# Small 32x32 products moved into the first chunk's chain, and the first stretch of a DeltaNet and feed-forward kernel written out with six joint bursts

## The chip, the cores and the metric

The kernel runs on one core of one Trainium2 chip. The metric is the device time of one execution in microseconds (us), lower is better. Four runs of the kernel before gave a median of 680.97 us, from 678.61 to 684.56.

A core has a matrix engine (PE; its weight loads are listed apart, as PEld), a vector engine (DVE), a scalar engine (ACT), a general engine (POOL) and a sync engine (SP), whose queue here issues nearly all DMAs. Each works through its own queue in order. Engines wait for one another by semaphores. PE writes to PSUM, and DVE or ACT read from there.

## What is computed

A delta-rule attention over 4 batches of 8 heads, 768 positions and 48 dimensions, followed by a feed-forward layer with a PReLU (384 to 2048 to 384) on its 3072 rows:

```
k_n = k / (norm(k) + 1e-06)
for t in range(S):
    y[:, :, t] = einsum('bhd,bhde->bhe', q[:, :, t], state)
    v_old = einsum('bhde,bhd->bhe', state, kt)
    state = state + bt * einsum('bhd,bhe->bhde', kt, vt - v_old)
x = y.transpose(0, 2, 1, 3).reshape(B * S, H * D)
h = x @ w_in
out = (maximum(h, 0) + alpha * minimum(h, 0)) @ w_out
```

## The kernel before

The sequence is cut into 12 chunks of 64 positions. A step n is one chunk for one pair of batches, so there are 24 steps and steps 2c and 2c+1 make up chunk c. Within a chunk the recurrence becomes a triangular system for each head. `grams(n)` (L407) forms the 64x64 matrix of k with k. Its 32x32 diagonal blocks are gathered for four steps at a time and inverted on DVE by an elimination (`eliminate`, L499 and L505, a long row of dependent small operations; it starts with POOL's L489). For the first four steps a shorter way is used: DVE eliminates 16x16 blocks only, and `cross` finishes the 32x32 inverses by products of 32x32 tiles on PE. `cross` is a generator in two halves. The first half runs L576 on PE (four products for each of its blocks) and copies the result from PSUM with ACT (L581). The second runs L586 (two for each block) and L593 (four), and DVE adds the results to `turned` and `inverse` (L600, L602). An argument `aside` is called between lots of products. Every product in float32 shows as two PE instructions in the trace.

From the inverses, `placing` (L631 on ACT or L627 on DVE) builds the tiles `diag` and `inv`. `between_1` (L663, then ACT's copy into `mid`, L669) and `between_2` (L677) join the two halves of each 64x64 inverse. `through_state` (L713, L718), `solve` (L743), `outputs` (L756), `next_state` (L772) and `to_ffn` (L795, three transposes, and ACT's copy into `xt`, L797) carry a step to its end. `flips` transposes k and q (L360) and copies them out with ACT (L381, L383).

The feed-forward layer of a chunk is dense work for PE: `ffn_in` has 48 products of 128x256 (L884), six for each of eight blocks that alternate between two PSUM banks (`ps_ffn`). After a block, ACT (L894) and DVE (L896, twice) read it out. Weights come in through staging space and are converted by ACT (L208, L209) and DVE (L218, L223); each converted piece is two parts of the generators `conv_in` and `conv_out`, and a finished piece frees its staging space for the next DMA (L192).

The order of work is written by hand. `weave` interleaves generators by shares, `part` takes a number of parts of one, and `now` runs what it is given at once. Before the first feed-forward work PE has only the chain of chunk 0. `busy(n)` (L1104) puts products there whose results are not used, 512 columns wide for each whole n; these are the fillers. All other PSUM work takes turns in three buffers of two banks (`ps_big`), so that a request waits for the readers of the buffer's last user.

Around the change: `first_chunk` runs the cross products of steps 0 and 1, then the chain of these steps with fillers in it and conversions (`convert`) beside it. After it, one `weave` runs the first hidden layer (`ffn_in(0)`), the cross products of steps 2 and 3 (with more of `ffn_in(0)` between their lots by `aside`), then `ready(2)` and `pair(2)`, the chain of steps 2 and 3, conversions, and `statics(4, 7)`, which prepares k for steps 4 to 7. A second `weave` then runs `ffn_in(1)` beside conversions, `statics(8, 9)` and the beginning of `eliminate(1)`. The products of the first output layer (L926) follow.

Of the kernel before, what the change touches and what calls it, by code (L numbers as in the profile page):

```python
# [41 lines left out]
def kernel(  # L42
# [83 lines left out]
    def load_q(n):  # L126
        if n < N:
            fetch(q, n, q_pad[n % NQ][:, :, 0:D])
# [6 lines left out]
    def load_late(n):  # L135

        if n < N:
            c, bp = steps[n]
            for t in range(2):
                src = k[2 * bp + t, :, c * C : (c + 1) * C, :]  # L140
                src = src.rearrange("(g a) p d -> a p g d", a=2)
                for a in range(2):
                    dst = k_late[n % NKL].rearrange("p (g a) d -> a p g d", a=2)
                    nc.sync.dma_start(out=dst[a][half(t ^ a), :, 0:D], in_=src[a])
# [246 lines left out]
    def now(pieces):  # L391
        for x in pieces:
            x()
# [310 lines left out]
    def through_state(n, p=None, p_y=None):  # L704
        if n >= N:
            return []
        c, bp = steps[n]
        if c == 0:
            rhs_[n] = by_parity(nv[n])
            return []  # L710
        p = region(p, G * (D + C), g=G)
        for g, a, t in quarters():
            nc.tensor.matmul(  # L713
                p[half(t ^ a), a, g], k_t[n][dims(a), g, half(t)], beside[bp][dims(a), t, g]
            )
        p_y = region(p_y, G * D, g=G)
        for g, a, t in quarters():
            nc.tensor.matmul(  # L718
                p_y[half(t), a, g], q_t[n][dims(a), t, g], state[bp][dims(a), t, g]
            )  # L720

        r = work.tile([128, 2, G, D], FP32, name="r")
        v_in = by_parity(nv[n])
        y = work.tile([128, H, D], FP32, name="y")
        rhs_[n], ys[n] = r, y

        def less(to, own, a):
            nc.vector.tensor_tensor(  # L728
                out=r[to, a], in0=v_in[to, a], in1=p[own, a, :, 0:D], op=ALU.subtract
            )  # L730

        return [
            lambda: less(slice(0, 128), slice(0, 128), 0),
            lambda: less(half(0), half(1), 1),
            lambda: less(half(1), half(0), 1),
            lambda: nc.scalar.copy(by_parity(y), p_y),  # L736
            lambda: masked(n, p[:, :, :, D : D + C]),
        ]

    def solve(n, p=None):  # L740
        p = region(p, G * D, g=G)
        for g, a, t in quarters():
            nc.tensor.matmul(  # L743
                p[half(t ^ a), a, g], inv[n % NE][half(t), a * G + g], rhs_[n][half(t), a, g]
            )
        us[n] = work.tile([128, 2, G, D], FP32, name="u")
        return [lambda: nc.vector.tensor_tensor(  # L747
            out=us[n], in0=p,
            in1=stats[n][1][:, 0:3:2, :, None].to_broadcast([128, 2, G, D]), op=ALU.mult,
        )]  # L750

    def outputs(n, p=None):
        c, bp = steps[n]
        p = region(p, G * D, g=G)
        for g, a, t in quarters():
            nc.tensor.matmul(  # L756
                p[half(t), a, g], a_t[n][half(t ^ a), a * G + g], us[n][half(t ^ a), a, g]
            )
        if c == 0:
            ys[n] = work.tile([128, H, D], FP32, name="y")  # L760
            return [lambda: nc.scalar.copy(by_parity(ys[n]), p)]
        return [lambda: nc.vector.tensor_tensor(
            out=by_parity(ys[n]), in0=by_parity(ys[n]), in1=p, op=ALU.add
        )]
# [329 lines left out]
            x()  # L1094
            yield

    PAIR = 6

    def busy(n, p=None):

        p = ps_one() if p is None else p
        while n > 0:
# [3 lines left out]
                k_t[NJ - 1].rearrange("p g i -> p (g i)")[0:ROWS, 0 : x.shape[-1]],  # L1106
            )
            n -= 1

    def pair(n):  # L1110

        both = (n, n + 1)
        for i in both:
            now(through_state(i))
        yield
        for i in both:
            now(solve(i))
            yield
        for i in both:
            now(outputs(i))  # L1120
            now(next_state(i))
            load_late(i + 2)
            load_v(i + 3)
            yield
        for i in both:
            to_ffn(i)
        yield

    READY = 5

    def ready(n):

        both = (n, n + 1)
        for i in both:
            place(i, (0,))
            flips(N, i)
            load_q(i + 2)
        yield
        for i in both:
            now(between_1(i))  # L1140
        yield
        for x in (1, 2, 3):
            for i in both:
                place(i, (x,))
        yield
        for i in both:
            now(between_2(i))
            scale_v(i)
            yield

    def queries():

# [15 lines left out]

        return mask

    def first_chunk(mask, convert):

        both = (0, 1)
        ahead[0] = n_in

        waits, pause = iter([0.5] * 2), []
        middle = cross(
            0, slice(0, 2 * H), edge, half_way, lambda: pause and busy(next(waits, 0), pause[0])
        )
        next(middle)  # L1180
        pause.append(ps_one())
        busy(1, pause[0])
        begin_in(6)
        for i in both:
            scale_v(i)
            mask(i)
        convert(2)
        next(middle)
        busy(1.25)
        place(0, (0,))  # L1190
        place(1, (0,), True)
        for i in both:
            place(i, (1,), True)
            now(between_1(i))
        busy(0.5, ps_ffn())
        for i in both:
            place(i, (2,))
            now(between_2(i))
        for i in both:
            now(through_state(i))  # L1200
            now(solve(i))
        busy(0.5, ps_ffn())
        now(outputs(0))
        convert(4)
        now(next_state(0))
        now(outputs(1))
        now(next_state(1))
        convert(4)
        busy(0.5, ps_ffn())
        for i in both:  # L1210
            to_ffn(i, ps_ffn())
            load_late(i + 2)
            load_v(i + 3)
        ahead[0] = FT * DM
        convert(2)

# [37 lines left out]
    fetch_out, _, conv_out = weights(pieces, stages, ids, out_done)  # L1254
    PARTS_OUT = 2 * len(pieces)

    def in_turn(*gens):
        for _ in range(CROSS):
            for g in gens:
                next(g)  # L1260
                yield

    def chain(*gens):
        for g in gens:
            yield from g
# [35 lines left out]
    def convert(n):  # L1301
        for _ in part(conv_in, n):
            pass

    first_chunk(mask, convert)
    fetch_out(SPACES)
    n = PARTS_IN - n + 10

    first_in = ffn_in(0)
    later = [  # L1310
        cross(0, slice(x * H, x * H + H), edge, half_way, lambda: next(first_in, None))
        for x in (2, 3)
    ]
    weave(
        (first_in, IN_PARTS - 10), (chain(in_turn(*later), ready(2), pair(2)), 2 * CROSS + READY + PAIR),
        (chain(conv_in, part(conv_out, 10)), n), (statics(NJ, 2 * NJ - 1), 2 * NJ + 1),
    )
    fetch_out(len(stages))
    blocks, SOON, LAST = eliminate(1), 12, 6
    weave(  # L1320
# [133 lines left out]
```

## Time and profile before

| | us |
|---|---|
| median of four runs | 680.97 |
| the four runs | 684.56, 678.61, 682.93, 679.00 |
| the profiled execution, its own time | 684.56 |
| its span, first to last instruction | 682.8 |
| mean granted PE clock | 0.984 |
| chain of chunk 0: the first L576 to the first L884 | 28.33 to 55.04 |
| first hidden layer, with steps 2 and 3: to the end of the last of its L884 | about 101.05 |
| second hidden layer: to the first L926 | 128.55 |

The costliest groups of instructions (busy us, mean ns of one; then idle time just before them and what ended most of it):

```profile
L884 PE MATMUL p_ffn<-xt,w_in 128*128 128x256 f32 x1152 | 265.2, 383 | 5.2 <-DVE act L896 2.3
L896 DVE SCALAR_TENSOR_TENSOR act<-act,al_t,p_ffn 128x256 f32<-128x256 f32 x176 | 76.5, 476 | 81.9 <-ACT act L894 81.9
L894 ACT ACTIVATE act<-p_ffn 128x512 f32<-128x512 f32 x88 | 52.4, 596 | 146.3 <-PE p_ffn L884 146.0
L505 DVE TENSOR_TENSOR block<-block,prod 128x30 f32<-128x30 f32 (+9 forms) x150 | 49.9, 333 | 5.1
```

A line names the line of the kernel, the engine, the operation, the tiles written and read, and how many. In lines in order of time (the timeline) the first two numbers are the start and the time from the first start to the last end, in us from the span's start; a bracket at the end gives the idle time before it and what ended that. PE's matrix products are pipelined, so their durations overlap; the distance from one start to the next tells their cost.

### The profile page before, as it was taken

To read this page: it belongs to the slowest core of one execution; us is meant where nothing else is said; L and a number is where in the kernel's file an instruction comes from. 1 tells how busy PE (TensorE), PEld (TensorE's weight loads), DVE (VectorE), ACT (ScalarE), POOL (GpSimd) and SP (SyncE) were. 2 spreads that over 40 slices of the span, in tenths; PEclk is the share of its full clock that TensorE was granted. 3 is DMA by queue.
4 is the path that set the end of the run, shared out by engine and by line. 5 is a ranking of instruction groups with operands and counts; after the bars stand their busy time and mean duration, and the time that the engine had idled before them with its cause. 6 is when DMAs were issued, how large, how long until landed. Compare 5 with 4: busy or idle time off the path is not lost.

```text
span 682.8 us, 21573 instructions
## 1 busy us (share of the span) xinstructions
PE 661.3 (97%) x9359; PEld 575.2 (84%) x9359; DVE 453.3 (66%) x1125; ACT 263.3 (39%) x624; POOL 35.6 (5%) x105
## 2 busy tenths in 40 slices
PE   6999998998999999999999999999999999999997
PEld 4587877766677998998998998998988989989997
DVE  4926688887989869757959757859656345354261
ACT  4815756415455334334334333332243134021110
POOL 6000111101000100001000000000000000000000
PEclk9859999999999999999999999999999999999999
DMA  8816864301342032022021111112111120100000
GB/s 128 238 47 177 202 157 116 90 24 25 66 89 38 13 72 48 11 62 48 15 49 36 23 40 36 26 36 37 25 43 31 30 42 2 29 9 2 23 1 25
DMA packets 110959, 37.69 MB, mean 55 GB/s; under 512 B 104160, under 2 KB 107248, under 8 KB 110864
## 3 DMA queue, kind: packets, MB, share of 16 engines
q1 hardware_dynamic: 109088, 35.81, 24.3%
q8 instruction: 74, 1.21, 0.7%
q10 hardware_dynamic: 1776, 0.49, 0.4%
q14 instruction: 21, 0.17, 0.1%
HBM read 31.56 MB, written 4.72 MB: 53 GB/s over the span
## 4 chain that ended last, share of the span: by engine, by line
PE 80%; DVE 13%; ACT 3%; DMA 1%; issue 1%; ACTq 0%; POOL 0%; SPq 0%; DVEq 0%
PE p_ffn L884 33%; PE p_ffn L948 27%; PE p_big L360 2%; PE p_big L663 2%; PE p_big L713 2%; PE p_big L743 2%; PE p_big L756 2%; DVE prod L499 2%; DVE block L505 2%; PE p_big L407 2%; PE p_big L677 2%; DMA ke<-in_k_dram 1%; DVE block L472 1%; PE p_big L718 1%; PE p_big L772 1%
## 5 line engine op out<-in xcount | busy, mean ns | idle before, releaser
L884 PE MATMUL p_ffn<-xt,w_in 128*128 128x256 f32 x1152 | 265.2, 383 | 5.2 <-DVE act L896 2.3
L884 PEld LDWEIGHTS p_ffn<-xt,w_in 128*128 128x128 f32 x1152 | 213.3, 190 | 35.2 <-ACT sums L894 2.2
L896 DVE SCALAR_TENSOR_TENSOR act<-act,al_t,p_ffn 128x256 f32<-128x256 f32 x176 | 76.5, 476 | 81.9 <-ACT act L894 81.9
L894 ACT ACTIVATE act<-p_ffn 128x512 f32<-128x512 f32 x88 | 52.4, 596 | 146.3 <-PE p_ffn L884 146.0
L948 PE MATMUL p_ffn<-w_out,act 128*128 128x192 f32 x480 | 82.5, 328 | 0.1
L948 PEld LDWEIGHTS p_ffn<-w_out,act 128*128 128x128 f32 x480 | 77.6, 190 | 1.1 <-issue 0.5
L505 DVE TENSOR_TENSOR block<-block,prod 128x30 f32<-128x30 f32 (+9 forms) x150 | 49.9, 333 | 5.1
L499 DVE TENSOR_TENSOR prod<-block 128x30 f32<-128x30 f32 (+9 forms) x150 | 48.9, 326 | 3.3 <-POOL block L489 1.6
L968 DVE TENSOR_TENSOR o_sb<-u,p_ffn 128x192 f32<-128x192 f32 x40 | 13.4, 353 | 52.2 <-PE p_ffn L948 41.9
L797 ACT COPY xt<-p_big 128x384 f32<-128x384 f32 x22 | 10.4, 477 | 75.7 <-PE p_big L795 75.7
L736 ACT COPY y<-p_big 128x384 f32<-128x384 f32 x22 | 10.5, 478 | 51.3 <-PE p_big L718 49.8
L948 PE MATMUL p_ffn<-space_out,sums 128*128 128x192 f32 x160 | 29.4, 327 | 0.0
L948 PE MATMUL p_ffn<-more,sums 128*128 128x192 f32 x160 | 29.3, 326 | 0.0
L948 PE MATMUL p_ffn<-w_out,sums 128*128 128x192 f32 x160 | 27.6, 326 | 0.0
L948 PEld LDWEIGHTS p_ffn<-more,sums 128*128 128x128 f32 x160 | 26.6, 190 | 0.0
L948 PEld LDWEIGHTS p_ffn<-space_out,sums 128*128 128x128 f32 x160 | 26.5, 190 | 0.1
L948 PEld LDWEIGHTS p_ffn<-w_out,sums 128*128 128x128 f32 x160 | 26.3, 190 | 0.0
L689 ACT COPY inv<-p_big 32x256 f32<-32x256 f32 x38 | 13.8, 363 | 29.4 <-DVE u L747 29.2
L631 ACT ACTIVATE diag<-inverse,which 64x128 f32<-64x128 f32 (+2 forms) x60 | 24.2, 405 | 2.1 <-DVE inverse L472 1.4
L728 DVE TENSOR_TENSOR r<-v_raw,p_big 64x192 f32<-64x192 f32 (+1 forms) x66 | 23.2, 352 | 1.0
L349 POOL TENSOR_TENSOR beta_t<-beta_t,rec 128x8 f32<-128x8 f32 x24 | 6.6, 275 | 308.7 <-DVE rec L347 288.1
L332 DVE TENSOR_REDUCE norm<-ksq 128x8 f32<-128x384 f32 x24 | 12.9, 546 | 13.8 <-ACT ksq L330 13.8
(156 smaller groups left out, 966.3 us busy)
## 6 DMA issues: line engine op xcount, KB each, us to landing
w_out<-in_moe_w_in_dram SPq DMA_DIRECT2D x12, 512.0 KB, 5.1
qp<-in_q_dram SPq DMA_DIRECT2D x48, 96.0 KB, 3.0
v_raw<-in_v_dram SPq DMA_DIRECT2D x48, 96.0 KB, 3.0
kl<-in_k_dram SPq DMA_DIRECT2D x96, 48.0 KB, 2.7
out_dram<-o_sb SPq DMA_DIRECT2D x92, 48.0 KB, 1.6
space_out<-in_moe_w_out_dram SPq DMA_DIRECT2D x11, 384.0 KB, 3.3
ke<-in_k_dram SPq DMA_DIRECT2D x43, 96.0 KB, 3.3
w_out<-in_moe_w_out_dram SPq DMA_DIRECT2D x5, 384.0 KB, 3.8
```

Source lines behind the costliest of these rows:

```text
L360: nc.tensor.transpose(p[0:ROWS, g * 128 : (g + 1) * 128], src[:, 2 * g : 2 * g + 2].rearrange("p h d -> p (h d)")[:, 0:ROWS], ident,)
L407: nc.tensor.matmul(p[half(t), a, g], k_t[n][dims(a), g, half(t)], k_t[n][dims(a), g, half(t)])
L499: nc.vector.tensor_tensor(out=prod, in0=r[:, 0:j, j : j + 1].to_broadcast([128, j, n]), in1=r[:, j : j + 1, j + 1 : HB].to_broadcast([128, ...
L505: nc.vector.tensor_tensor(out=r[:, 0:j, j + 1 : HB], in0=r[:, 0:j, j + 1 : HB], in1=prod, op=ALU.add)
L631: nc.scalar.mul(out, x, which[rows, i : i + 1])
L663: nc.tensor.matmul(p[half(t ^ a if changes(n) else t), a, g], right[n % EARLY][half(t), a * G + g : a * G + g + 2].rearrange("p b i -> p ( ...
L689: nc.scalar.copy(to[rows], p[rows])
L728: nc.vector.tensor_tensor(out=r[to, a], in0=v_in[to, a], in1=p[own, a, :, 0:D], op=ALU.subtract)
L884: nc.tensor.matmul(p_h[:, i], w_in[:, t, (f + i) * 128 : (f + i + 1) * 128], xt[:, t], start=(t == 0), stop=(t == KT - 1),)
L894: nc.scalar.activation(g, p_h, ACT.Relu, scale=-1.0)
L896: nc.vector.scalar_tensor_tensor(out=g[:, i], in0=g[:, i], scalar=al_t[:, f + i : f + i + 1], in1=p_h[:, i], op0=ALU.mult, op1=ALU.add,)
L948: nc.tensor.matmul(p, x(i), w(i), start=(i == 0), stop=(i == FP - 1))
```

## The change

Three fillers of half a filler product each (256 columns) are taken out of `first_chunk`, and the four halves of the cross products of steps 2 and 3 are put in: the first half of each in the places of two fillers, the second half of step 2's in the place of the third, and the second half of step 3's after `to_ffn`. The `weave` that ran the first hidden layer is replaced by `second_pair`, which writes the order out: six groups of small products, each of which joins what belonged to two steps or to a step and a gram, with 5, 5, 6, 7, 7, 6 and 12 parts of the hidden layer after them. The flips of steps 4 and 5 and of the queries of steps 2 and 3 come before the first part. `through_state`, `solve`, `outputs` and `next_state` of the two steps share PSUM buffers. `pair`, `ready` and `in_turn` are dropped. The number of products, conversions and loads stays as it was, apart from the fillers.

```diff
-    def first_chunk(mask, convert):
+    def first_chunk(mask, convert, halves):
...
             place(i, (1,), True)
             now(between_1(i))
-        busy(0.5, ps_ffn())
+        next(halves[0])
         for i in both:
             place(i, (2,))
             now(between_2(i))
         for i in both:
             now(through_state(i))
             now(solve(i))
-        busy(0.5, ps_ffn())
+        next(halves[1])
         now(outputs(0))
         convert(4)
         now(next_state(0))
         now(outputs(1))
         now(next_state(1))
         convert(4)
-        busy(0.5, ps_ffn())
+        next(halves[0])
         for i in both:
             to_ffn(i, ps_ffn())
             load_late(i + 2)
             load_v(i + 3)
+        next(halves[1])
...
-    first_chunk(mask, convert)
+    first_chunk(mask, convert, [
+        cross(0, slice(x * H, x * H + H), edge, half_way) for x in (2, 3)
+    ])
     fetch_out(SPACES)
...
-    later = [
-        cross(0, slice(x * H, x * H + H), edge, half_way, lambda: next(first_in, None))
-        for x in (2, 3)
-    ]
-    weave(
-        (first_in, IN_PARTS - 10), (chain(in_turn(*later), ready(2), pair(2)), 2 * CROSS + READY + PAIR),
-        (chain(conv_in, part(conv_out, 10)), n), (statics(NJ, 2 * NJ - 1), 2 * NJ + 1),
-    )
+    convert_on = chain(conv_in, part(conv_out, 10))
+
+    def alongside(products, pieces, *gens):
+        weave((part(first_in, products), products), (part(convert_on, pieces), pieces), *gens)
+
+    def second_pair():
+
+        n = 2
+        both, x = (n, n + 1), NJ
+        squares(x)
+        squares(x + 1)
+        for i in range(2):
+            place(n + i, (0,))
+            flips(x + i, n + i)
+            load_early(x + i + NKE)
+            load_q(n + i + 2)
+        now(weigh(x))
+        now(weigh(x + 1))
+        alongside(5, 3)
+        for i in both:
+            now(between_1(i))
+        now(grams(x))
+        squares(x + 2)
+        alongside(5, 3, (chain(*(placing(i, (1, 2, 3)) for i in both)), 6))
+        for i in both:
+            now(between_2(i))
+        now(grams(x + 1))
+        for i in both:
+            scale_v(i)
+        flips(x + 2, N)
+        load_early(x + 2 + NKE)
+        now(weigh(x + 2))
+        alongside(6, 3)
+        y = ps_big()
+        pieces = []
+        for i in range(2):
+            pieces += through_state(n + i, None, y[:, :, i * G * D : (i + 1) * G * D])
+        now(pieces)
+        squares(x + 3)
+        alongside(7, 3)
+        y = ps_big()
+        pieces = []
+        for i in range(2):
+            pieces += solve(n + i, y[:, :, i * G * D : (i + 1) * G * D])
+        now(pieces)
+        now(grams(x + 2))
+        flips(x + 3, N)
+        load_early(x + 3 + NKE)
+        now(weigh(x + 3))
+        alongside(7, 3)
+        pieces = []
+        for i in both:
+            y = ps_big()
+            pieces += outputs(i, y[:, :, 0 : G * D]) + next_state(i, y[:, :, G * D : 2 * G * D])
+        now(pieces)
+        for i in both:
+            load_late(i + 2)
+            load_v(i + 3)
+        alongside(6, 3)
+        for i in both:
+            to_ffn(i)
+        now(grams(x + 3))
+        alongside(IN_PARTS - 36, 4)
+
+    second_pair()
```

## The prediction

> **What bounds the kernel now.** I read the page first: engine totals, then the chain that ended last.
>
> ```profile
> PE 661.3 (97%) x9359; PEld 575.2 (84%) x9359; DVE 453.3 (66%) x1125; ACT 263.3 (39%) x624; POOL 35.6 (5%) x105
> ...
> PE 80%; DVE 13%; ACT 3%; DMA 1%; issue 1%; ACTq 0%; POOL 0%; SPq 0%; DVEq 0%
> ```
>
> PE (the matrix engine) is 97% busy and carries 80% of the chain, so work or waiting taken off PE in the changed stretch should reach the end unless another engine holds it there. Next I read busy times by stage (columns: PE, PEld, DVE, ACT, POOL, granted clock, DMA share, GB/s). The stages are: chain up to the first filler that goes, rest of the chain, first hidden layer, second hidden layer.
>
> ```profile
> 28.33:43.88 15.55, 15.55 (x395) 11.15 (x395) 8.09 (x20) 5.16 (x10) 0.00 (x0) 0.55 0.40 88
> 43.88:55.04 11.16, 10.54 (x269) 9.06 (x269) 5.94 (x13) 3.05 (x8) 0.00 (x0) 0.71 0.16 43
> 55.04:101.05 46.01, 45.14 (x1023) 35.33 (x1023) 31.77 (x80) 29.67 (x67) 6.31 (x16) 1.00 0.75 186
> 101.05:128.55 27.50, 25.03 (x181) 21.05 (x181) 24.27 (x70) 16.08 (x34) 4.24 (x10) 1.00 0.41 104
> ```
>
> ACT has 29.67 and DVE 31.77 of 46 us in the third stage, so neither binds on average; their order may. The clock is low in the first two. One-microsecond slices give 0.94 at 29–30, 0.50 from 30 to 50 and 0.82 at 50–51: half speed from 29.9 to 50.4. Then PE in order of time, the three fillers of the change and the first W_in product:
>
> ```profile
> 43.80 1.22 PE L1104 MATMUL p_ffn<-k_t,ident 112*128 112x256 f32 x2
> 44.95 3.52 PE L677 MATMUL p_big<-diag,mid 64*64 64x32 f32 x62
> ...
> 50.24 0.74 PE L1104 MATMUL p_ffn<-k_t,ident 112*128 112x256 f32 x2
> ...
> 53.06 0.70 PE L1104 MATMUL p_ffn<-k_t,ident 112*128 112x256 f32 x2
> ...
> 55.04 0.70 PE L884 MATMUL p_ffn<-xt,w_in 128*128 128x256 f32 x2 [0.62 <-ACT xt L797]
> ```
>
> And the stretch after it:
>
> ```profile
> 56.04 0.70 PE L884 MATMUL p_ffn<-xt,w_in 128*128 128x256 f32 x2
> 56.67 0.44 PE L576 MATMUL p_big<-turned,sums 32*32 32x16 f32 x32
> 57.04 0.70 PE L884 MATMUL p_ffn<-xt,w_in 128*128 128x256 f32 x2
> ...
> 62.26 0.68 PE L586 MATMUL p_big<-act,inverse 32*32 32x16 f32 x32
> ...
> 78.64 1.12 PE L677 MATMUL p_big<-diag,mid 64*64 64x32 f32 x32 [0.22 <-ACT diag L631]
> ...
> 86.21 1.00 PE L713 MATMUL p_big<-beside,k_t 48*64 48x112 f32 x32 [0.65 <-DVE right L413]
> ...
> 109.54 2.83 PE L884 MATMUL p_ffn<-xt,w_in 128*128 128x256 f32 x12 [1.85 <-ACT sums L894]
> ```
>
> Each lot of 32x32 products sits between W_in products, and PE waits in four places (last bracket). The wait at 109.54 is DVE's: its L896 stands behind L499 of the elimination, which waits for POOL's L489 until 108.19.
>
> **Part 1: fillers out, 32x32 products in.** A W_in product (two PE instructions) costs 0.44 us back to back (24 instructions from 121.96 to 127.24: 5.28). From 56.04 to 57.04 are one product and one lot: the lot costs 1.00-0.44 = 0.56, though its own work is 0.37 (chain row); the switch between shapes is some 0.17. An L586 lot costs 62.87-60.34-4x0.44 = 0.77. Eight lots at 0.56 and two at 0.77: **6.0 us leave the stretch.** The fillers' chain rows, 1.15, 0.67 and 0.63, free 2.45.
>
> What comes in: 64 instructions of L576 at half clock, by 1.83 for 128 of L593 there (0.92; if they ran like L586 there, 0.97 for 32, it were 1.9): I take 0.95, since L576 uses four quadrants as L593 does. The second 64 at full clock, 2x0.37 and a switch: 0.85. Twice 32 of L586 and 64 of L593, 0.61+2x0.37: 2.7, with a switch 2.8. **Sum 4.6.**
>
> New wait: the third set needs a PSUM buffer that L780 on DVE reads. L780 stands behind two conversions and ended at 53.5 and 54.0; PE would be there at 53.1. I take 0.4 (bounds 0 and 0.9). PE queues the transposes of y behind it. In return the xt copies on ACT (54.13 to 55.0) lie under the fourth set and 16 transposes (L360), which move ahead of the first W_in product; PE's 0.74 us gap there goes. First W_in product: 53.1+0.4+1.4+0.7+1.4+1.75 = **58.75**, with all 32x32 products and both steps' flips done.
>
> **Part 2: six joint bursts.** L663, L677, L407, L713/718, L743 and L756/772 formed eleven bursts among W_in products; now six. Five switches at 0.17: **0.85 saved**. The W_in count (48) and conversions (22 halves) are the same. The waits at 78.64 (0.38 with its pipeline end) and 86.21 (0.65) go. L887–L897's work is unchanged. On SP the loads of q move from 71.9 to about 60, ahead of ke loads that land well before use; loads of kl move behind w_out pieces and are needed a chunk later: nothing. POOL keeps its order: nothing.
>
> But ACT's queue changes. Between the xt copies (end about 56.3) and the copy into diag that step 3's L677 needs stand 8 conversion halves at 0.70 (start to start 54.87 to 55.59), 3 squares at 0.43, 4 flip copies at 0.47, 5 placements at 0.42, 4 norms at 0.23, two mid copies at 0.35, one L894 at 0.5, two L652 at 0.2: 13.4 us, so **69.7**. The copy for step 2 is done 2.65 earlier, at 67.05. PE has from 58.75: five products 2.2, L663 and L407 2.55, five products 2.2, two switches: ready at 66.0. It waits 1.05, runs L677 for 1.1, and waits 1.55 until 69.7: **2.6 us of new wait** where before it was 0.38. Bounds: 0, if ACT keeps ahead, and 4, if it also waits for DVE's norms. From 70.65 follow 38 products (16.8), L407 three times (1.9), L713/718 (2.7), L743 (1.25), eight L360 (0.95), L756/772 (2.15), L795 (0.65), five switches (0.85): the first hidden layer ends at 97.9, not 101.05.
>
> **Given back or kept later.** The last gram now has twelve products behind it before the second hidden layer, not four, so the elimination's start on DVE and POOL moves by more than PE: the same rows one after another put L499 at 104.15, not 108.19 (-4.0). PE loses 0.55 and 1.3 waiting for L896 around it, against 0.62 and 2.0 now. The third block of the layer starts at 105.45, not 109.54; past it the order is the same.
>
> **Sum.** Off: 2.45+6.0+0.85, gaps 0.74+0.38+0.65, and 0.8 around the elimination: 11.9. On: 4.6+0.4+2.6 = 7.6. Net **-4.2**, and -4.1 by the walk; I take -4.1. The profiled execution took 684.56 (span 682.8, 1.8 around it), so 680.5 there. It is the slowest of four; their median is 680.97. On that scale: **676.9**.
>
> **The clock, against the change.** Between 53.5 and 58.75 PE would run only 32x32 products and transposes. The row: the clock fell at 29.9, after a stretch (26.5 to 29.9) of 0.64 us of filler, 1.22 idle and 1.5 of L576. Yet it stayed up in 84.5 to 87.9, with some 0.3 of dense work and 1.9 of 48x64 products. So a fall near 57 is possible, not certain.
> The Trainium skill, "TensorE: Matmul & The Clock Gate", section "What's actually happening", has the clock judged in windows of about 3.4 us, half after an idle one; the 20.5 us of half clock here are six such. By it a single fall would cost 1.7 us as an estimate.
> The same page, section "Part 4: PE-mode transpose", says that transposes do not count as PE work in the same way, which speaks against this change; no run here shows it.
>
> **Rivals.** (a) *The clock falls near 57.* L360 took 1.03 for four at half clock against 0.44, a 128x256 product 1.15 against 0.63. Flips and the first five products then add 3.8, or 6 if L663 is slow too; 2.6 of it lies under ACT's wait, so the cost is 1.3 to 3.3. With 2: 678.9.
> (b) *Slower: the clock does not rise at 50.4*, because the filler at 43.9 no longer helps. L756/772 then cost 3.7 instead of 2.15 (L407's 1.13 against 0.62), the two last sets 4.0 instead of 2.8, L795 1.5, flips 4.1: with five slow products some 8.4, less 2.6 under ACT's wait: +5.9, so +1.8 net: 682.8. It decides once PE comes to the second L677 after 73.7. For it: fillers are what filled the chain. Against: in the 3.4 us before the rise PE ran L677 and L743 alone.
> (c) *The gain is swallowed at the elimination*: L499 stays near 107–108 because DVE (24.27 of 27.5 us busy) gets no earlier: 0 to -1.5, 680.2. Against: DVE idled 14 of 46 us in the stretch before.
> (d) *ACT does not bind*: another -2.6, 674.3. For it: before, ACT waited 3.23 us for PE in this stretch. Against: the sum of rows.
> That the change does something else is excluded: the built order has no such fillers and six bursts.
>
> **How the numbers follow.** Forecast 0.45, (d) 0.15, (a) 0.20, (c) 0.10, (b) 0.10. The four runs before spread by 6 us, so a median of few moves by 2 either way. Range 672.5 (d, less 2) to 683 (b). One per cent, about what a measurement can tell from no change, is 6.8 us: faster than 674.2 needs (d) or a lucky forecast, 0.20; slower than 687.8 needs more than (b), 0.06; within, 0.74.
>
> **What would show it.** Right: first L884 at 58 to 59.5 with clock 1.0; PE waits of 1 to 1.6 us before each L677, released by ACT's L631; L499 about 4 us earlier. Wrong: half clock past 51 (b) or after 57 (a); no wait at L677 (d); L499 within 1 us of 108 (c).

## The result and the profile after

The changed kernel took 682.63 us (median of 43 runs, 679.86 to 687.29); the kernel before, on the same chips, 679.47 us (64 runs, 677.00 to 685.83). The ratio is 1.0037, 95% interval 1.0025 to 1.0049: a loss of some 2.5 us, small but clear of the noise, where 4.1 us of gain was forecast. Three runs of the experiments below, each over 1.5% slower than the fastest of its kernel, are left out of the ratios and mean clocks. The profiled execution took 680.9 us, with a span of 679.2.

The page of the changed kernel first: the engines' totals, PE's instruction queue (packets, MB, share), and the chain that ended last.

```profile
PE 655.7 (97%) x9353; PEld 576.4 (85%) x9353; DVE 454.4 (67%) x1125; ACT 264.2 (39%) x624; POOL 35.0 (5%) x105
...
q8 instruction: 74, 1.21, 0.7%
...
PE 80%; DVE 11%; ACT 3%; SPq 2%; issue 2%; DMA 1%; POOL 0%; POOLq 0%
```

PE's share of the chain is what it was. "issue" has gone from 1% to 2%: that is time in which an engine waited for nothing that the profile shows, and stops of PE are among it. The queue line will explain them: 74 packets of 16 KB each, 1.21 MB in all, bring PE's instructions. The trace has 2 x 9353 products and weight loads of PE and 209 other instructions of its queue, nearly all on semaphores: 18915 in all, so a packet is a block of some 256.

Busy times by stage (the same columns as before the change). The kernel before in two profiles, that of the prediction and a second one taken later, whose clock was full all through; then the changed kernel. In each the first row runs from the first L663 to the first L884 (the rest of the first chunk's chain), the second to the first L926. (In the second profile of before the first row begins 0.22 us ahead of its first L663, at 37.25, so the chain is 12.24 us there.)

```profile
40.25:55.04 14.79, 14.17 (x334) 12.63 (x333) 5.94 (x13) 3.42 (x9) 0.00 (x0) 0.66 0.12 34
55.04:128.55 73.51, 70.17 (x1202) 56.38 (x1203) 56.05 (x149) 45.75 (x101) 10.54 (x26) 1.00 0.62 155
```

```profile
37.03:49.49 12.46, 10.31 (x333) 8.83 (x332) 7.13 (x17) 3.58 (x10) 0.00 (x0) 1.00 0.31 101
49.49:122.97 73.48, 70.34 (x1203) 56.55 (x1203) 55.80 (x148) 45.95 (x101) 10.48 (x26) 1.00 0.61 150
```

```profile
36.49:59.99 23.50, 19.51 (x662) 18.30 (x663) 11.48 (x27) 7.91 (x18) 0.00 (x0) 0.72 0.46 132
59.99:124.77 64.78, 62.46 (x867) 53.30 (x867) 52.16 (x136) 41.74 (x92) 9.96 (x26) 0.97 0.58 144
```

The stretch gave what was forecast and a little more: 73.5 to 64.8, -8.7 us. The chain took it all back: +8.7 against the first profile of before (14.79), +11.3 against the second (12.24). PE is idle for 4.0 of its 23.50 us, and its clock is 0.72 there. Past the first L926 all three profiles take the same 554.2 to 554.4 us. PE of the changed kernel in order of time, in this chain, shows the idle time (bracket):

```profile
36.49 2.06 PE L663 MATMUL p_big<-diag,right 64*64 64x32 f32 x64 [0.42 <-ACT diag L631]
38.47 0.73 PE L576 MATMUL p_big<-turned,sums 32*32 32x16 f32 x64
39.13 1.06 PE L677 MATMUL p_big<-diag,mid 64*64 64x32 f32 x29
41.73 1.19 PE L677 MATMUL p_big<-diag,mid 64*64 64x32 f32 x33 [1.54 <-issue]
...
45.95 0.72 PE L576 MATMUL p_big<-turned,sums 32*32 32x16 f32 x37 [0.78 <-issue]
...
50.97 0.66 PE L593 MATMUL p_big<-inverse,act 32*32 32x16 f32 x56
53.22 0.24 PE L593 MATMUL p_big<-inverse,act 32*32 32x16 f32 x6 [1.59 <-issue]
53.39 1.40 PE L795 MATMUL p_ffn<-ident,y 128*128 128x128 f32 x6
...
56.54 1.10 PE L360 MATMUL p_big<-ident,ke 128*112 128x128 f32 x4
...
59.99 2.53 PE L884 MATMUL p_ffn<-xt,w_in 128*128 128x256 f32 x10
```

Three times PE stops inside a burst, in the middle of products of one kind that all have their operands: 1.54, 0.78 and 1.59 us, 3.9 in sum. Counted from the start of the program, with PE's matrix products, weight loads and semaphore instructions together, the first instruction after each stop is number 1473, 1729 and 2241. Each leaves 193 when divided by 256 ("193 modulo 256"), so they follow the fifth, sixth and eighth end of a block. In the trace's DMA records the fifth, sixth and eighth packet of PE's instruction queue land at 40.29, 44.47 and 51.97, and PE goes on 1.43, 1.48 and 1.25 us later. What ends each stop is the arrival of its block. One-microsecond slices around the first and the third stop (same columns; the clock is the third number from the end):

```profile
40.00:41.00 1.00, 0.19 (x7) 0.07 (x3) 0.00 (x0) 0.33 (x1) 0.00 (x0) 1.00 0.00 0
41.00:42.00 1.00, 0.28 (x9) 0.28 (x10) 0.00 (x0) 0.00 (x0) 0.00 (x0) 1.00 0.00 0
42.00:43.00 1.00, 1.00 (x50) 1.00 (x49) 0.42 (x1) 0.00 (x0) 0.00 (x0) 1.00 0.00 0
43.00:44.00 1.00, 0.92 (x47) 0.82 (x42) 0.90 (x2) 0.00 (x0) 0.00 (x0) 0.67 0.06 16
...
52.00:53.00 1.00, 0.00 (x0) 0.00 (x0) 0.96 (x3) 0.00 (x0) 0.00 (x0) 1.00 0.00 0
53.00:54.00 1.00, 0.78 (x10) 0.76 (x10) 0.77 (x3) 0.00 (x0) 0.00 (x0) 0.79 0.62 106
```

After each of these two the clock falls: half from 43.3 to 50.2 and again from 53.6 to 60.4. A third fall, 70.7 to 74.1, lies in the stretch, behind a wait of 0.94 us for ACT. Nor is the low clock one execution's chance. The mean clock over the changed kernel's runs is 0.983 and never above 0.990; of 107 runs of the kernel before in the comparisons below 49 were at 0.997 or more, with a mean of 0.995. Half clock goes with time: the runs of before at 0.997 or more have medians of 678.2 to 678.8 us, those below 0.990 some 684 (681.4 in one comparison). By (1 - clock) x 2 x 680 the mean clocks are 23 us of half clock a run against 7, and over the runs of either kernel one us of it goes with 0.2 to 0.3 us of time: 3 to 5 us. Continued to no half clock at all, the straight line through the changed kernel's runs comes to 677.8 us, those through the four sets of runs of before to 678.2 to 678.9. By this estimate the two kernels would take about the same at full clock, and the loss goes with the clock. The profile of before that the prediction was read from (clock 0.984, 684.56 us) was thus of the rarer kind: 20 of the 107 are below 0.990.

### The profile page after: what moved, and what is told of

It is laid out like the page before. It is cut to its first block, busy times and chain, and to the rows that moved or that the text cites. A ratio compares the mean times of both kernels' runs of the same rounds, so it can differ in the third digit from the quotient of the medians.

```text
span 679.2 us, 21569 instructions
## 1 busy us (share of the span) xinstructions
PE 655.7 (97%) x9353; PEld 576.4 (85%) x9353; DVE 454.4 (67%) x1125; ACT 264.2 (39%) x624; POOL 35.0 (5%) x105
## 3 DMA queue, kind: packets, MB, share of 16 engines
q8 instruction: 74, 1.21, 0.7%
## 4 chain that ended last, share of the span: by engine, by line
PE 80%; DVE 11%; ACT 3%; SPq 2%; issue 2%; DMA 1%; POOL 0%; POOLq 0%
PE p_ffn L884 32%; PE p_ffn L948 27%; PE p_big L360 3%; PE p_big L713 2%; PE p_big L756 2%; PE p_big L743 2%; DVE prod L499 2%; PE p_big L663 2%; DVE block L505 2%; PE p_big L1102 2%; PE p_big L677 2%; SPq L120 1%; PE p_big L718 1%; PE p_big L772 1%; PE p_big L407 1%
## 5 line engine op out<-in xcount | busy, mean ns | idle before, releaser
L884 PE MATMUL p_ffn<-xt,w_in 128*128 128x256 f32 x1152 | 261.4, 383 | 3.4 <-DVE act L896 2.5
L884 PEld LDWEIGHTS p_ffn<-xt,w_in 128*128 128x128 f32 x1152 | 216.0, 191 | 33.9 <-ACT act L894 3.1
L499 DVE TENSOR_TENSOR prod<-block 128x30 f32<-128x30 f32 (+9 forms) x150 | 48.9, 326 | 3.3 <-POOL block L489 1.6
L780 DVE TENSOR_TENSOR beside<-beside,p_big 48x384 f32<-48x384 f32 (+1 forms) x36 | 19.8, 550 | 2.9 <-PE p_big L772 2.7
L713 PE MATMUL p_big<-beside,k_t 48*64 48x112 f32 x704 | 21.3, 259 | 0.0
```

The source lines that it names most:

```text
L499: nc.vector.tensor_tensor(out=prod, in0=r[:, 0:j, j : j + 1].to_broadcast([128, j, n]), in1=r[:, j : j + 1, j + 1 : HB].to_broadcast([128, ...
L713: nc.tensor.matmul(p[half(t ^ a), a, g], k_t[n][dims(a), g, half(t)], beside[bp][dims(a), t, g])
L780: nc.vector.tensor_tensor(out=x, in0=x, in1=p[rows], op=ALU.subtract)
L884: nc.tensor.matmul(p_h[:, i], w_in[:, t, (f + i) * 128 : (f + i + 1) * 128], xt[:, t], start=(t == 0), stop=(t == KT - 1),)
```

## The experiments

The theory formed from the traces: PE's instructions arrive in blocks of 256, and where it uses them up faster than they come (128 products with their 128 loads take 1.4 us in L576 and, by 64 in 2.0, some 4 us in L677 at full clock) it stops at the end of a block. The change adds 640 short instructions to the chain, two and a half blocks, and the stops bring the clock down with them. The rivals: the half fillers kept the clock up and are missed; products that use little of the array lower the clock; the joint stretch is itself no gain; the stops belong to some place and not to a count.

**The parts alone.** First the four halves of `cross` in the chain, the three half fillers out, and the order of the stretch as before:

```diff
-        busy(0.5, ps_ffn())
+        next(halves[0])
...
-        (first_in, IN_PARTS - 10), (chain(in_turn(*later), ready(2), pair(2)), ...
+        (first_in, IN_PARTS), (chain(ready(2), pair(2)), READY + PAIR),
```

> The four halves of the 32x32 products in the chain, the old order of the stretch after it. Theory S (PE's instruction supply: blocks of 256 PE instructions, and the chain uses them up faster than they arrive): the loss is here, 1.004 to 1.010 of before, with PE stalls of 0.7 to 1.6 us inside bursts, at every 256th instruction. Rival J (the written-out order with joint bursts costs, by its waits for ACT): part 1 alone is a gain, 0.993 to 0.997.

682.55 us; ratio 1.0051 (1.0025 to 1.0077), mean clock 0.983. This part alone loses as much as the whole change. Its profile has two stops in the chain, in the same bursts as the changed kernel's first and third:

```profile
41.98 2.02 PE L677 MATMUL p_big<-diag,mid 64*64 64x32 f32 x34 [1.05 <-issue]
54.62 0.29 PE L593 MATMUL p_big<-inverse,act 32*32 32x16 f32 x6 [2.35 <-issue]
```

Then the rest of the change: the chain with its fillers as before, the lots of steps 2 and 3 among ten W_in products, the six joint bursts.

```diff
-        next(halves[0])
+        busy(0.5, ps_ffn())
...
-        alongside(IN_PARTS - 36, 4)
+        alongside(IN_PARTS - 46, 1)
...
+    weave((chain(*(part(g, 1) for g in later), ...), 4), (part(convert_on, 3), 3))
     second_pair()
```

> Fillers and the chain as before, the 32x32 products of steps 2 and 3 with ten hidden-layer products between their lots, then the written-out order with six joint bursts. Theory S: the order itself is worth its fewer switches and gaps less ACT's wait, 0.997 to 1.001, no stall inside a burst of the chain. Rival J: 1.003 or more, with waits of 1 us or more before each L677.

684.39 us; 1.0035 (0.9998 to 1.0071), clock 0.990: inconclusive. It shows no gain by itself, though its two runs with a clock of 1.0 took 676.45 and 677.56 us, against the 678.6 of before at 0.997 or more. In its profile two stops (0.46 and 0.53 us) now fall into the lots of steps 2 and 3, which stand closer together than in the kernel before.

**Are the fillers missed?** The three half fillers out of the kernel before, and nothing in their place:

```diff
-        busy(0.5, ps_ffn())
```

> Before without its three half fillers in the chain, nothing in their place. Rival K (the fillers hold the clock up, and their loss is what costs): 1.003 or more, and half clock for longer than before. Theory S: their own 1.6 to 2.4 us are saved in part, since PE then waits for ACT and DVE there, 0.997 to 1.000.

680.14 us; 0.9987 (0.9959 to 1.0016), clock 0.993 against 0.994 for before. They are not missed. Nor do they help when they are put back, into the changed kernel behind three of the halves:

```diff
         next(halves[0])
+        busy(0.5, ps_ffn())
```

> The changed kernel with the three half fillers kept, each behind the half that took its place. Rival K: the clock stays up and the time falls below the changed kernel's, 0.996 to 1.001 of before. Theory S: the fillers give the instruction supply 0.6 us each, stalls shrink by about as much as the fillers take, 1.002 to 1.006 of before.

683.31 us; 1.0055 (1.0028 to 1.0083), clock 0.986. Stops of 0.38 and 1.85 us remain. By both, the rival of the missing dense work falls.

**The kernel before once more**, for a profile at full clock.

> The kernel before, for a second profile: most of its runs show a mean granted clock of 0.995 and more, the first profile 0.984. All theories: L884 of the first hidden layer starts 5 to 8 us earlier than 55.04 if the clock holds, and the first L926 at 122 to 125. Theory S: with the chain at full clock one or two stalls of some 1 us appear at 256-instruction marks even here.

678.95 us. It gave the stages shown above, and stops in its own chain too:

```profile
38.56 1.25 PE L663 MATMUL p_big<-diag,right 64*64 64x32 f32 x34 [0.19 <-issue]
46.75 0.37 PE L756 MATMUL p_big<-u,a_t 64*64 64x48 f32 x9 [1.03 <-issue]
```

Numbers 1217 and 1729: 193 modulo 256 again. The first profile of before has none. At half clock PE eats its instructions more slowly (L677 took 3.52 us there, 2.00 here), so the prediction was read from the one kind of execution that hides this cost.

**The supply by itself.** The first fillers replaced by 256 products of 32x32 by 16 columns, 1024 instructions, whose results are not used:

```diff
-    busy(BUSY)
+    for x in range(64):
+        for i in range(4):
+            nc.tensor.matmul(p[quad(i), x % 32], ident[quad(i), quad(i)], ident[...])
```

> Before with the eight wide fillers, where PE waits for the elimination anyway, replaced by 256 products of 32x16 (1024 PE instructions, results unused): measures the supply by itself. Theory S: they take 12 to 16 us, with a stop of 1 to 2.5 us at every 256th instruction. Without a limit of supply: 6 us, by 128 in 1.54, and no stops.

699.12 us (one run). PE in order of time:

```profile
25.32 1.90 PE L1298 MATMUL p_big<-ident 32*32 32x16 f32 x128 [3.09 <-issue]
30.42 1.90 PE L1298 MATMUL p_big<-ident 32*32 32x16 f32 x128 [3.20 <-issue]
33.88 1.90 PE L1298 MATMUL p_big<-ident 32*32 32x16 f32 x128 [1.55 <-issue]
37.88 0.30 PE L1298 MATMUL p_big<-ident 32*32 32x16 f32 x7 [2.10 <-issue]
```

Runs of exactly 128 products and 128 loads, 1.90 us of work at half clock (it rose at 66.7 us only), then 1.55 to 3.20 us of nothing: from start to start 3.5 to 5.1 us a block. The DMA records show where the time goes. The fetch of each such block begins 1.1 to 2.8 us after PE has gone into the block before, takes 1.0 to 1.3 us, and PE goes on 1.3 to 1.5 us after the landing. This is the price of a block that nothing hides.

**Many short or few long, in the fillers' places.** Unused products in place of the three half fillers, the real ones left in the stretch: first 112 of 32x32 by 16 columns (448 instructions), then, in place of these, 11 of 32x32 by 512 columns (44; the second diff is against the first). The sets behind the transposes of y, which the expectations name, were not built.

```diff
-        busy(0.5, ps_ffn())
+        tiny(32)
```

> Before with its three half fillers replaced by as many 32x16 products as the changed kernel has there, results unused (32, 32, 48 products, and 48 behind the transposes of y), and the real ones left in the stretch. Theory S: stalls of 1 us and more appear in the chain and the mean clock falls to 0.980 to 0.987 as in the changed kernel; 1.006 to 1.012. Rival K (only missing dense work lowers the clock): as the kernel without fillers, clock 0.993, 1.002 to 1.005 for the added work.

```diff
-                nc.tensor.matmul(p[quad(i), b], edge[quad(i), 2 * H + b], turned[0][...])
+            nc.tensor.matmul(p[x], ident[x, x], src[x])
```

> The same places filled with 32x32 products of 512 columns (3, 3, 5, and 5 behind the transposes; 32 PE instructions in all instead of 640), as long as the small ones within some tenths of a us and with as little of the array in use. Theory S: no added stall, clock 0.992 or more, 1.000 to 1.004. Rival A (it is the little of the array in use that lowers the clock, not the number of instructions): clock 0.980 to 0.987, 1.004 to 1.009.

The short ones: 692.46 us, 1.0163 (1.0137 to 1.0190), more than expected, clock 0.984. The long ones: 681.64 us, 1.0033 (1.0011 to 1.0056), clock 0.994 as before. The chain of the first has a stop of 1.31 us in L756 and one among the added products, shown here; the chain of the second has only the one in the second row:

```profile
55.92 0.30 PE L1115 MATMUL p_ffn<-turned,sums 32*32 32x16 f32 x6 [3.51 <-issue]
```

```profile
45.53 0.49 PE L756 MATMUL p_big<-u,a_t 64*64 64x48 f32 x17 [0.30 <-issue]
```

Both use tiles of 32x32. The long ones take more time than the fillers (4.0 us against 2.1), which is about their ratio, and leave the clock alone. So small tiles by themselves do not lower it; with many short instructions, and their stops, it is lower.

**Count or place?** 64 unused products early, to move every later instruction along the count:

```diff
-    busy(BUSY)
+    tiny(64)
+    busy(BUSY - 0.5)
```

> The changed kernel with 64 unused 32x16 products (128 instructions, counting weight loads and multiplications) ahead of the fillers that lie behind the queries' products, and half a filler less there, so that every later instruction is counted 128 higher. Theory (PE's instructions come in blocks of 256, and it stops where a block ends): the stops move 128 instructions up the program, to the counts 1473, 1729, 1985 and 2241 again, which now lie in the first L576 burst or the end of L663, in L743, in L756/L772 and in the L586/L593 set after it; no stop stays at the 30th L677, the 28th L576 or the 57th L593. Their sum stays between 2 and 4.5 us, and the time with them: ratio to the kernel before 1.002 to 1.007, mean clock of the runs below 0.989. Rival (the stops belong to these bursts: a PSUM bank, an operand, a wait that the profile does not show): they stay at the 30th L677, the 28th L576 and the 113th instruction of L593, whatever the count.

> The kernel before without the three half fillers, with the same 64 unused products ahead of the first fillers and half a filler less there. Theory: the block ends move from L663, L743 and the second L756 (0.28, 0.26 and 1.11 us of stops without the shift) to the first half of L663 or L677 and to the first L756, and the fifth one out of the chain into W_in products; four block ends in the chain instead of five. Stops of 0 to 1.2 us instead of 1.65; first W_in product within 0.5 us of where it would be without them; ratio 0.995 to 1.000. Rival (stops belong to places): 1.65 us of stops at the same lines and ratio 0.9987 as without the shift.

A product is two multiplications and two loads, so 64 were 256 instructions, not 128: a whole block, and the ends of blocks fell on the same places as without them. The added products also write over a part of the first chunk's products of queries and keys before these are masked, so that both kernels compute something else there, with the same work in the same order. The times: 685.71 us, 1.0100 (1.0065 to 1.0136), and 682.81 us, 1.0069 (1.0039 to 1.0099). Of the three old places of the changed kernel only the third stopped again (number 2497, 1.25 us). What is new is a stop in the added products themselves, behind those of the queries (the kernel without fillers):

```profile
26.15 0.30 PE L1156 MATMUL p_ffn<-ident 32*32 32x16 f32 x7 [4.33 <-issue]
```

3.63 us in the other, both at number 705. Count or place was left open. Half as many in the middle of the first fillers, in their buffer, settled it:

```diff
+    p = ps_one()
+    busy(BUSY / 2, p)
+    tiny(32, p)
+    busy(BUSY / 2 - 0.5, p)
```

> The changed kernel with 32 unused 32x16 products in the middle of the first fillers and half a filler less there. A 32x16 product is two multiplications and two weight loads, so these are 128 instructions, half a block of 256 (the 64 of the shifted kernels were 256, a whole block, so there the block ends fell on the same places as without them). Theory (PE stops where a block of 256 instructions ends): the stops are again at counts of 193 modulo 256 and so at new places: the end of the L663/L576 set, L743, L756/L772, L586/L593 near their start and the second L593 set; none at the 30th L677, the 28th L576 or the 113th instruction of the L593 set. Ratio to the kernel before 1.001 to 1.007, mean clock below 0.990. Rival (the stops belong to the places): one at each of the three old places, at counts of 65 modulo 256.

685.45 us; 1.0077 (1.0050 to 1.0104), clock 0.982. PE in the chain:

```profile
37.26 0.53 PE L593 MATMUL p_big<-inverse,act 32*32 32x16 f32 x30 [1.54 <-issue]
...
44.69 3.52 PE L677 MATMUL p_big<-diag,mid 64*64 64x32 f32 x62
...
49.97 1.05 PE L576 MATMUL p_big<-turned,sums 32*32 32x16 f32 x64
...
58.45 0.82 PE L593 MATMUL p_big<-inverse,act 32*32 32x16 f32 x44 [1.06 <-issue]
```

L677 and L576 run through, the third old place too, and the stops are at numbers 1217 and 2497, both 193 modulo 256, in other bursts: the first in the products of steps 0 and 1, the second in the last set of L593. All 36 stops inside a burst that the profile puts down to "issue", from 20 to 85 us in all the profiles of this study, are at 193 modulo 256. The stops go by the count, and each ends 1.2 to 1.6 us after the packet of the same number has landed. Not every end of a block stops, and the expectation named some bursts that ran through. In all 17 traces, at over 1200 ends of blocks, PE never goes into a block sooner than 1.2 us after its packet has landed; where the packet came early enough, PE runs through.

> The kernel before without the three half fillers, with the same 32 unused products in the middle of the first fillers. Theory: stops only at counts of 193 modulo 256; the ends of blocks move to L586 or its filler, L593, the first part of L677 and the first L756/L772, and one leaves the chain. Stops of 0 to 1.2 us in sum against 1.65 without the shift; ratio 0.995 to 1.000, clock 0.993 or more. Rival (places): stops in L663, L743 and the second L756 as without the shift, ratio 0.9987.

The same in the kernel without fillers: 682.45 us, 1.0029 (1.0006 to 1.0052), clock 0.989. One stop of 1.54 us at number 1217 instead of 1.65 us in three. The expected gain did not come: the one stop lies earlier (35.2 to 36.8), and the clock is half from 36.4 to 50.1, nearly to the end of the chain.

**Half the dose.** Only the first two sets (L576) in the chain; L586 and L593 among six W_in products behind it:

```diff
-        next(halves[0])
-        next(halves[1])
...
+    aside[0] = lambda: next(first_in, None)
+    weave((chain(*(part(g, 1) for g in halves)), 2), (part(convert_on, 2), 2))
     second_pair()
```

> The changed kernel with only the first two sets (the L576 products, 256 instructions) in the chain; the L586 and L593 sets stand among six W_in products behind it, ahead of the joint bursts. Theory (each block of 256 instructions added to the chain costs a stop of 1 to 2 us and, through the clock, as much again): between the kernel before and the changed one, ratio 0.999 to 1.003, mean clock 0.985 to 0.992, stops of 1 to 2.5 us in the chain. Rival (the stretch of 32x32 products and transposes without dense work between 50 and 60 us is what lowers the clock, and the first two sets cost nothing): half clock no later than 51 us, mean clock of the runs 0.993 or more and the ratio at most 0.998, as the prediction's gain in the stretch then shows.

681.17 us; 1.0028 (1.0006 to 1.0049), clock 0.988, stops of 0.48, 1.05 and 0.39 us: between the two kernels, as the theory had it, though the interval holds the changed kernel's 1.0037 too.

**The joint stretch with neither the halves nor the fillers in the chain** (the second kernel above, less its three half fillers):

```diff
-        busy(0.5, ps_ffn())
```

> The part of the change that needs no products in the chain: the three half fillers out, the chain otherwise as before; then the 32x32 products of steps 2 and 3 among ten W_in products, and the six joint bursts. Theory (the chain's added instructions are the loss; leaving out the fillers costs nothing): ratio 0.996 to 1.001, mean clock 0.990 or more; L926 (the elimination's end) by 1 to 2 us earlier than with the fillers in the same program. Rival (the joint stretch itself is no gain: ACT's queue or the clock after it gives back what the shape switches save): 1.002 or more, with the clock's mean at 0.988 as with the fillers.

680.75 us; 1.0008 (0.9977 to 1.0040), clock 0.986. Inconclusive: neither the clock of the theory (0.990) nor the time of the rival (1.002).

**Does a stop by itself lower the clock?** The kernel before, with ACT's first copy into `diag` made five times (same values), so that PE waits before L663 with no instruction added to it:

```diff
+        for _ in range(5):
             place(0, (0,))
```

> The kernel before with ACT's first copy into diag made five times (same values) ahead of L663, so that PE idles there about 1.7 us longer, with no instruction more on PE. Theory 1 (any stop of this length in the chain lowers the clock, as the stops at block ends would): PE's idle time before L663 is 1.5 to 2.2 us; half clock afterwards in most runs, mean clock 0.990 or less, ratio 1.004 to 1.008. Theory 2 (the stop costs itself only, and what lowers the clock is the longer run of short instructions): mean clock 0.993 or more, ratio 1.002 to 1.003. If the clock lies between, both have a part.

683.34 us; 1.0051 (1.0027 to 1.0076), mean clock 0.9905 against 0.9954 for before. None of its 12 runs is above 0.994; 13 of the 25 of before are at 0.997 or more. The wait, and the slices behind it:

```profile
38.59 2.23 PE L663 MATMUL p_big<-diag,right 64*64 64x32 f32 x64 [2.38 <-ACT diag L631]
```

```profile
39.00:40.00 1.00, 1.00 (x42) 1.00 (x40) 0.00 (x0) 0.24 (x1) 0.00 (x0) 1.00 0.07 16
40.00:41.00 1.00, 1.00 (x25) 0.94 (x22) 0.00 (x0) 0.27 (x2) 0.00 (x0) 0.66 0.00 0
41.00:42.00 1.00, 1.00 (x4) 0.35 (x6) 0.00 (x0) 1.00 (x3) 0.00 (x0) 0.50 0.00 0
```

The wait is 2.2 us longer than in before (0.22), and the kernel is 3.7 us slower by the medians. So a stop costs its own length and, through 6.8 us of half clock (40.3 to 47.1), something like half as much again: in the profile the chain behind the wait, from the first L663 to the first L884, took 13.7 us with 0.2 of stops in it, against 12.2 with 1.2 of stops at full clock. The interval of the ratio (1.8 to 5.2 us) doesn't fix this second part; the clocks of the runs do show it.

No kernel here beats the kernel before: the best, 0.9987 without the fillers, has 1 in its interval.

## Why the prediction was wrong

The change went the other way than forecast. That the time still lies in the stated range is luck: the upper end, 683, stood there for rival (b), a clock that does not rise, and not for what happened. Step by step:

- *"Sum 4.6" for the 32x32 products that come in.* **This step failed.** It priced 640 instructions by the time that PE works on them, in part by rows at half clock. With their operands there and PE free, they also need to be fetched, a wait that the sum puts at nothing. From first start to the next burst the four sets took 0.66, 2.03, 2.94 and 1.82 us, 7.5 in sum, 2.4 of it stops; a third stop, of 1.54, fell into L677. In all the profile has 3.9 us of stops in the chain; before at full clock has 1.2. The forecast had the first W_in product at 58.75, 18.5 us after the first L663; it came 23.5 us after.
- *The clock.* The forecast let the chain warm up at 50.4 and stay warm, and gave (a), a fall near 57, a chance of 0.20 at 2 us, and (b), no rise, 0.10. Half clock came in all runs (none is above 0.990), in the profile from 43.3, 53.6 and 70.7. The first two falls lie behind stops, which neither rival had. The 16 transposes of L360 took 3.45 us there at half clock, for 1.75 in the forecast. The doubt that transposes don't count as work for the clock is not borne out: it rose at 60.4, after 3.41 us in which PE ran these transposes alone but for the last 0.4. "Fillers are what filled the chain", the argument for (b), is refuted; without them the clock is 0.993. In the chain of the profile 13.2 us were at half clock, (1 - 0.72) x 2 x 23.50, where the forecast had 10.2 (40.25 to 50.4).
- *The fillers' 2.45 us and the lots' 6.0 us off; 0.85 for switches; the gaps.* Right in sum. The lots alone gave 5.5 (in the profile of the first part alone the first L884 is at 58.14 and the first L926 at 126.13, 68.0 us for 73.5). The fillers' 2.45 were read in part at half clock; at full clock they take 1.8. First L884 to first L926 fell by 8.7 us; the forecast is -4.1 less the +3.7 of the chain (18.5 against 14.8), -7.8.
- *0.4 us for L780, "bounds 0 and 0.9".* It was 0: PE came later. The xt copies did lie under the fourth set; the wait of 0.62 before the first L884 is gone.
- *"2.6 us of new wait" for ACT before the two L677.* Its mechanism was right, its size was 0.9; PE came later, ACT's queue had gone on meanwhile. That is 1.7 us better than forecast. The third fall, behind this wait, took some 1.5 of it back: four L360 and twelve instructions of L884 took 4.6 us from 71.06 to 75.69, for 3.1 by the forecast's costs.

```profile
69.35 1.06 PE L677 MATMUL p_big<-diag,mid 64*64 64x32 f32 x29 [0.94 <-ACT diag L631]
...
105.76 2.83 PE L884 MATMUL p_ffn<-xt,w_in 128*128 128x256 f32 x12 [0.46 <-DVE sums L896]
```

- *The elimination (rival c).* Not swallowed: its first L499 is at 104.42 (forecast 104.15, before 108.19) and the third block of the second hidden layer at 105.76 (105.45, before 109.54), the wait before it 0.46 for 1.85. These absolute times agree only because L663 started 3.8 us earlier in this profile than in that of before, which made up for the chain's loss.
- *The base.* The chain was read from an execution at half clock, where blocks arrive in time and short products look slow. Against the full-clock profile the chain grew by 11.3 us.

In sum, from the first L663 on the two profiles differ by +8.7 - 8.7 + 0.2 = +0.2 us instead of -4.1; against the full-clock profile by 11.3 - 8.7 + 0.2 = +2.8, about what the ratio has. By the rows, the sets (+7.5) and the transposes (+3.5) are new there, the fillers (-1.8) are gone, L677 with L743 takes 2.2 more, 1.5 of it a stop, and the rest cancels. How much of the 11.3 is half clock was not measured apart. Nor was a version of the changed order without stops found, so that its gain is shown only for the stretch, not for the whole.

The Trainium skill, "Runtime: NRT & Kernel Launch", section "Instruction fetch mechanics", has blocks of 16 KiB, 256 instructions, refilled from a queue of the sequencer's own while it executes, with room for 2048 on PE, and calls the crossing mostly hidden. The blocks agree with these runs; for short products "mostly hidden" doesn't: 0.8 to 1.6 us each in the changed kernel's chain, up to 4.3 us in one of the others, and in the run of short products alone a stop at every block, which does not look like 2048 instructions in store.

## What to carry to other kernels

Moving small products out of dense work into a serial chain moves their instructions too: count them (a float32 product here is four) and ask, for each 256, whether long instructions lie ahead that hide the fetch. "issue" inside a burst of equal instructions, at equal distances in the count, is the sign; and a stop in a chain can cost more than its length, as the clock can fall behind it. Before a chain is priced, take the profile of more than one execution, and price it from one whose clock is the usual one.

## What the runs showed of the hardware

- PE can stop at every 256th instruction where those around it are short: 1.55 to 3.20 us in a run of 32x32 by 16 products alone, 0.2 to 4.3 us among others. What it waits for is the block: in these traces it went into none sooner than 1.2 us after the landing. The block of the changed kernel's first stop was fetched from 39.4 to 40.3, and PE went on at 41.7.
- A window need not be idle to bring the clock down. Half clock lasted 6.8 us, two times 3.41, after the first and the third stop of the changed kernel and after the late copy, and 3.41 us in the changed kernel's third fall. In the 3.41 us before the falls PE was busy for some 1.9 us (to 43.3), 1.8 us (to 53.6) and 2.5 us (to 70.7) in the changed kernel, and 1.7 us (to 40.3) with the late copy: 50 to 72%. The busy share alone does not decide it: in the second profile of before PE was busy for 2.3 of the 3.41 us from 45.6 to 49.0, 67%, and the clock stayed full. The Trainium skill, "TensorE: Matmul & The Clock Gate", section "What's actually happening", has windows of 3.4 us, which agrees, and the clock halved after an idle one, which is stricter than what these four show.
